# The second MLP in three 768-token tiles, both of its products by block sums

## Chip, cores and metric

One core of one Trainium2 chip runs the kernel. The time is device microseconds of the whole kernel, from one launch, and its median over the runs; less is better. TensorE multiplies, VectorE, ScalarE and GpSimd work on elements, SyncE issues the DMAs.

## What is computed

Windowed attention over 4 sequences of 576 positions and 8 heads, then two MLPs of width 512 and inner width 2048 over all 2304 tokens:

```python
x = attention(q, k, v).transpose(0, 2, 1, 3).reshape(2304, 512)
h = x @ w_in;  r = max(h, 0);  x = (r * r) @ w_out            # first MLP
h = x @ w2_in; g = h * (1 / (1 + exp(-h))); out = g @ w2_out  # second MLP
```

All of it has to hold to nearly 32-bit precision. The weights arrive as 64-bit floating point, and the kernel itself turns them into 32-bit.

## The kernel before

**Precision.** TensorE multiplies in a rounded 32-bit type. Each operand is therefore split into a rounded part (hi, a cast) and the remainder (lo, a subtraction), and a product is three matmuls: hi x hi, hi x lo, lo x hi.

**Block sums.** In the first product of an MLP, `mlp2` (line 971) takes 512 tokens and two 128-row blocks of the inner width (a pair f, eight pairs in all) as a 2 x 2 by 2 x 2 block product and forms it from seven products of block sums instead of eight products of blocks. The blocks and sums of the weights are called a11, a12, a22 and s1 to s4, those of the tokens b11, b21, b22 and t1 to t4. Each of the seven is 2 x 3 matmuls of 256 columns (line 999). The seven lie in four banks of PSUM, and VectorE and ScalarE add them up into a tile `h` (lines 1013 and 1015). A 256-token tile takes eight plain products instead.

**Second product.** After a pair's sums come the nonlinearity (lines 1035 to 1041), the split of `g` (lines 371 and 378) and, one pair later, the plain second product: per block c 12 matmuls of the tile's whole width (lines 1053 to 1055), which accumulate over all sixteen blocks in four banks y0 to y3.

**Tiles and stages.** The first MLP has three tiles of 256 tokens (beside attention) and three of 512, the second four of 512 and one of 256. `weights` (line 381) converts one block of weights: load, six or so element operations (lines 405 to 441), split. `sums` (line 466) forms s1 to s4. Blocks and sums of the first product go to DRAM and are streamed back for every tile by `stream` (line 512); the second product's weights stay in sixteen resident buffers `w1`. `load_x` (line 919) loads and splits a tile's tokens and forms t1 to t4 (line 966).

**Order.** A planner (`Planner.order`) simulates five engines with fixed costs and gives every operation its engine and its place in that engine's queue, by a key (a due time in units of one block for 256 tokens). All DMAs go through SyncE's queue in the planned order; a DMA that waits for a buffer holds up those behind it. SBUF is handed out in pages: 28 of 4 KB per partition (`u4`), 8 and 2 of 2 KB, beside the sixteen `w1` and two `blk`.

Of the kernel before, what the change touches and what calls it, by code (L numbers as in the profile page):

```python
# [27 lines left out]
P = 128  # L28
# [12 lines left out]
HOLDS = {"w0": "u4", "wa": "u4", "ws": "u4", "wb": "u4", "wc": "u2", "h": "u4", "xr": "u4", "xo": "u2", "cw": "u2", "raw": "u4", "ap": "u4", "x": "u4", "x2": "u4", "xn": "u2", "g4": "u4", "st": "u4",  # L41
         "g2": "u2", "cv": "u2", "r": "u3", "yo": "u2", "stg": "u2"}
# [40 lines left out]

class Buf:


    def __init__(self, tags, make, psum):
        self.tags, self.make, self.psum = tags, make, psum
        self.alloc_op = self.tile = self.pages = None
        self.last = {}  # L90
# [13 lines left out]
class Op:  # L104
    def __init__(self, engines, fn, deps, key, allocs, uses):
# [6 lines left out]
        self.pace, self.full, self.lock, self.kind = False, True, False, 0  # L112
# [4 lines left out]
class Planner:  # L117
# [7 lines left out]
    def __init__(self):  # L125
        self.ops, self.slots = [], {}

    def buf(self, tags, make, psum=False):

        for g, n in tags.items():  # L130
            self.slots.setdefault(g, [Page() for _ in range(n)])
        return Buf(list(tags), make, psum)
# [10 lines left out]
    def order(self):  # L143
        after, left, users = {}, {}, {}
        pace = sorted((o for o in self.ops if o.pace), key=lambda o: o.key)
        for o in self.ops:
# [3 lines left out]
            need = set(o.deps)  # L150
# [6 lines left out]
        slots = self.slots  # L157
# [10 lines left out]
        def at(o, e, t):  # L168
            for g, k in o.wants:
                x = [p.free.get(e, 0.0) for p in slots[g] if not p.held]  # L170
                if len(x) < k:
                    return None
                t = max(t, min(x) if k == 1 else sorted(x)[k - 1])
# [12 lines left out]
        def take(b, e):  # L186
            b.pages = [min((p for p in slots[g] if not p.held), key=lambda p: p.free.get(e, 0.0)) for g in b.tags]
            for p in b.pages:
                p.held = True

        def drop(b):
            f = {e: max(t + self.SYNC[x, e] for x, t in b.last.items()) for e in free}
            for p in b.pages:
                p.held, p.free = False, f

# [17 lines left out]
        def fill(until):  # L213

            while free["PE"] + 0.25 < until:
# [10 lines left out]
                take(b, "PE")  # L226
# [11 lines left out]
        while left_n:  # L238
# [32 lines left out]
            for b in o.allocs:  # L271
                take(b, e)
# [48 lines left out]
class Kern:  # L321
    def __init__(self, ctx, tc, qkv, w1, w2, out):
# [3 lines left out]
        self.sb = pool("sb")  # L326
        self.ps = pool("ps", space=bass.MemoryType.PSUM)
        self.dr = pool("dr", space=bass.MemoryType.DRAM)
        self.pl = Planner()
# [8 lines left out]

    def buf(self, tag, bufs, cols, dt=F32, rows=P):
        return self.pl.buf({tag: bufs}, lambda: self.sb.tile([rows, cols], dt, tag=tag, name=tag, bufs=bufs))  # L340

    def spot(self, use, cols, dt=F32):

        pool, most = HOLDS[use], MOST[use]
        bufs, words = POOLS[pool]
        words //= 2 if dt == I64 else 1
        return self.pl.buf({use: most, pool: bufs}, lambda: self.sb.tile(
            [P, words], dt, tag=pool, name=use, bufs=bufs)[:, :cols])
# [32 lines left out]
    def weights(self, m, c, key, dkey, js=(0, 1)):  # L381
# [3 lines left out]
        for j in js:  # L385
            raw = self.spot("raw", n, I64)
            cv = self.spot("cv", n)
# [939 lines left out]
```

## Time and profile before

| | |
|---|---|
| median of 3 runs | 891.92 us (890.57 to 892.31) |
| span of the profiled execution | 894.6 us |
| TensorE busy, share of the span | 875.7 us, 98% |
| VectorE | 647.2 us, 72% |
| ScalarE | 425.0 us, 48% |
| GpSimd | 107.9 us, 12% |
| moved by DMA | 217.33 MB, 243 GB/s |

The span is that of the execution that was profiled, from its first to its last instruction; that execution's own time outside the profiler is not given, and the median is that of other runs. The second MLP begins at about 502 us. A matmul's row is longer than the distance to the next one, since matmuls overlap; the pace is read from the distance between starts.

### The profile page before, as it was taken

The page shows a single profiled execution, that of the slowest core. Times are in us where ns is not written, and L with a number is a line of the kernel's source. Part 1 is how long each engine was busy: PE and PEld are TensorE (multiplying, and loading weights), DVE is VectorE, ACT ScalarE, POOL GpSimd, SP SyncE. Part 2 cuts the span into 40 slices and gives each one's busy share as a digit, 9 for nine tenths or more (in the row PEclk, how much of TensorE's full clock was granted, in tenths as well). Part 3 has the DMA queues.
Part 4 walks back from the last instruction along what each step waited for, and adds up shares of the span by engine and source line. Part 5 has one row for each costly group of instructions (what it writes and reads, how often), then busy time and mean ns, then how long its engine had stood idle before and what let it go on. Part 6 is the DMA issues. An engine that isn't in the chain of part 4 may idle for free.

```text
span 894.6 us, 17795 instructions
## 1 busy us (share of the span) xinstructions
PE 875.7 (98%) x6511; PEld 798.8 (89%) x6511; DVE 647.2 (72%) x1652; ACT 425.0 (48%) x1113; POOL 107.9 (12%) x125
## 2 busy tenths in 40 slices
PE   8999999999989999999999999999999999999998
PEld 6889899999877888989999988999999999999998
DVE  7999999788786997776788999684557445545322
ACT  5978888777455365432333364342233222323222
POOL 2242233111311010010110012000002000000000
PEclk9999999999999999999999999999999999999999
DMA  6887685579898988966787897956575556634050
GB/s 259 279 268 270 212 308 200 193 273 323 287 301 310 340 322 299 346 213 238 235 282 260 329 329 268 325 196 236 165 240 206 172 188 219 260 141 164 25 212 25
DMA packets 75735, 217.33 MB, mean 243 GB/s; under 512 B 8576, under 2 KB 20096, under 8 KB 75648
## 3 DMA queue, kind: packets, MB, share of 16 engines
q1 hardware_dynamic: 75648, 216.20, 69.2%
q8 instruction: 51, 0.84, 0.4%
q14 instruction: 36, 0.29, 0.1%
HBM read 170.03 MB, written 46.14 MB: 242 GB/s over the span
## 4 chain that ended last, share of the span: by engine, by line
PE 68%; DVE 16%; DMA 7%; issue 4%; ACT 3%; POOL 1%; SPq 0%; DVEq 0%; POOLq 0%; ACTq 0%
PE s L999 28%; PE y L1053 10%; PE y L1054 10%; PE y L1055 10%; DMA raw<-w 4%; DVE ap L625 2%; DMA x<-xo 1%; DVE cv L441 1%; DVE g L378 1%; PE s L851 1%; DVE cv L437 1%; DVE h L1015 1%; PE s L853 1%; PE s L852 1%; DVE w L378 1%
## 5 line engine op out<-in xcount | busy, mean ns | idle before, releaser
L1015 DVE TENSOR_TENSOR h<-s,h 128x512 f32<-128x512 f32 x224 | 139.4, 622 | 127.5 <-PE s L999 117.1
L1053 PE MATMUL y<-g,w 128*128 128x512 f32 (+1 forms) x512 | 194.7, 380 | 1.1 <-ACT yo L371 1.0
L1054 PE MATMUL y<-g,w 128*128 128x512 f32 (+1 forms) x512 | 192.8, 377 | 1.0 <-DVE g L378 1.0
L1055 PE MATMUL y<-g,w 128*128 128x512 f32 (+1 forms) x512 | 192.7, 376 | 0.0
L999 PE MATMUL s<-x,ws 128*128 128x256 f32 x1344 | 171.9, 283 | 0.1
L999 PEld LDWEIGHTS s<-x,ws 128*128 128x128 f32 x1344 | 165.8, 192 | 0.7 <-DVE h L1015 0.3
L371 ACT CAST g<-r 128x512 fp32r<-128x512 f32 (+1 forms) x175 | 94.1, 542 | 72.4 <-DVE r L1035 41.9
L378 DVE TENSOR_TENSOR g<-r,g 128x512 fp32r<-128x512 f32 (+1 forms) x172 | 102.8, 613 | 21.8 <-ACT g L371 18.3
L1055 PEld LDWEIGHTS y<-g,w 128*128 128x128 f32 x512 | 96.2, 188 | 18.3
L1053 PEld LDWEIGHTS y<-g,w 128*128 128x128 f32 x512 | 96.2, 188 | 17.4 <-ACT yo L371 1.6
L1054 PEld LDWEIGHTS y<-g,w 128*128 128x128 f32 x512 | 96.3, 188 | 16.4 <-DVE g L378 1.3
L999 PEld LDWEIGHTS s<-x,wa 128*128 128x128 f32 x768 | 99.8, 191 | 5.8 <-ACT xo L371 1.1
L999 PE MATMUL s<-x,wa 128*128 128x256 f32 x768 | 103.8, 284 | 1.0 <-ACT xo L371 0.9
L1039 ACT ACTIVATE r<-h 128x512 f32<-128x512 f32 x64 | 37.1, 624 | 121.5 <-DVE h L1015 121.4
L633 ACT ACTIVATE ap<-ap,ast 96x128 f32<-96x128 f32 (+3 forms) x168 | 61.8, 370 | 19.0 <-DVE ast L625 18.9
L427 POOL TENSOR_SCALAR raw<-raw 128x512 f32<-128x512 f32 x40 | 39.2, 982 | 179.1 <-ACT cv L405 88.7
L1013 ACT COPY h<-s 128x256 f32<-128x256 f32 x56 | 20.8, 371 | 80.8 <-PE s L999 79.0
L851 PE MATMUL s<-x,w 128*128 128x256 f32 x192 | 57.1, 297 | 0.2 <-DVE ast L625 0.2
L1041 DVE TENSOR_TENSOR r<-h,r 128x512 f32<-128x512 f32 x64 | 41.7, 687 | 20.2 <-ACT r L1039 20.2
L852 PE MATMUL s<-x,w 128*128 128x256 f32 x192 | 54.7, 285 | 0.2 <-DVE x L378 0.2
L853 PE MATMUL s<-x,w 128*128 128x256 f32 x192 | 54.5, 284 | 0.0
L413 ACT ACTIVATE raw<-raw 128x512 int32<-128x512 uint32 x59 | 40.2, 681 | 25.2 <-DMA raw<-w 25.1
(144 smaller groups left out, 1442.5 us busy)
## 6 DMA issues: line engine op xcount, KB each, us to landing
raw<-w SPq DMA_DIRECT2D x64, 512.0 KB, 6.1
ws<-w2x SPq DMA_DIRECT2D x64, 512.0 KB, 5.3
ws<-w1x SPq DMA_DIRECT2D x48, 512.0 KB, 6.0
wa<-w2s SPq DMA_DIRECT2D x40, 512.0 KB, 4.5
wa<-w1s SPq DMA_DIRECT2D x24, 512.0 KB, 5.9
w1s<-w SPq DMA_DIRECT2D x16, 512.0 KB, 4.1
w1x<-st SPq DMA_DIRECT2D x16, 512.0 KB, 3.4
w2s<-st SPq DMA_DIRECT2D x16, 512.0 KB, 4.8
```

Of the source, the lines that this page charges most:

```text
L371: self.nc.scalar.copy(out=out, in_=in_)
L378: self.eng[eng].tensor_tensor(out=out, in0=a, in1=b, op=ALU.subtract)
L633: es.append(self.op({"ACT": c_act(nk) + 0.185}, lambda e, i=i, n=n, c=c, p=p, st=st: nc.scalar.activation(out=p.tile[:n, c], in_=p.tile[:n ...
L851: nc.tensor.matmul(o, wh.tile[:, s], xh, start=(kk == 0), stop=False)
L852: nc.tensor.matmul(o, wh.tile[:, s], xl, start=False, stop=False)
L853: nc.tensor.matmul(o, wl.tile[:, s], xh, start=False, stop=(kk == KC - 1))
L999: nc.tensor.matmul(bank.tile[:, o:o + 256], wp, xp, start=i == 0, stop=last, skip_group_check=True)
L1015: add = lambda o, a, b: nc.vector.tensor_tensor(out=o, in0=a, in1=b, op=ALU.add)
L1041: b = self.op({"DVE": c_dve(n)}, lambda e, r=r, src=src: nc.vector.tensor_tensor(out=r.tile, in0=src(), in1=r.tile, op=ALU.mult), [a], k, ...
L1053: nc.tensor.matmul(o, wh.tile[:, s], gh.tile, start=c == 0, stop=False)
L1054: nc.tensor.matmul(o, wh.tile[:, s], gl.tile, start=False, stop=False)
L1055: nc.tensor.matmul(o, wl.tile[:, s], gh.tile, start=False, stop=(c == NF - 1))
```

## The change

The second MLP runs in three tiles of 768 tokens, in blocks of 384. Its second product is formed from seven products too. A tile is two phases (`strassen`, new): first the first product of all eight pairs, each with its nonlinearity, into sixteen buffers `gq`; then the second product, one of the seven products after the other, each over all eight pairs. The seven no longer lie apart and are added up outside: products chain in their bank. A2 goes on in A1's bank after A1's result has been copied out, A3 and A4 after that, B2 in B1's; what has to be added from another bank is added on the way out. The block sums of `g` are formed in place in the second phase, and each is split just ahead of its product into one of ten buffers `hl`.

The second product's weights are converted with a narrower first block, over about twice the stretch; their sums s1 to s4 are formed (`sums2`, new), stored to DRAM and streamed back in every tile (`stream2`, new); a11, a12 and a22 stay resident (`wp`). `load_xs` (new) loads and splits the tokens of a 768-token tile and forms the differences in place. SBUF is one area in pieces of 256 words (`Area`, `put`), where the new buffers get any free place, from its low or its high end. The keys of the second MLP's weight conversions are set anew.

```diff
-TILES = ([(0, 256), (256, 256), (512, 256), (768, 512), (1280, 512), (1792, 512)], [(0, 512), (512, 512), (1024, 512), (1536, 512), (2048, 256)])
-
-POOLS = {"u4": (28, 1024), "u2": (8, 512), "u3": (2, 512)}
+TILES = ([(0, 256), (256, 256), (512, 256), (768, 512), (1280, 512), (1792, 512)], [(0, 768), (768, 768), (1536, 768)])
+POOLS = {"u2": (8, 512), "u3": (2, 512), "u4": (28, 1024), "w1": (16, 1024), "blk": (BLK_BUFS, 1280)}
...
+    def put(self, place, dt, name):
+
...
+        if at > self.ring_at:
+            self.ring.tile([P, at - self.ring_at], F32, name="gap")
+        self.ring_at = at + words
+        return self.ring.tile([P, words // (2 if dt == I64 else 1)], dt, name=name)
...
+            late = m and j
+            wide = n if not late or c % 2 else n // 2
             both = (self.spot("st", 2 * n, F32R) if m and not j else self.spot("w0", 2 * n, F32R) if j == 0 else
-                    self.buf("w1", NF, 2 * n, F32R))
+                    self.spot("wp" if c < 2 * KEPT else "sq", 2 * wide, F32R) if late else self.buf("w1", NF, 2 * n, F32R))
...
+            if late:
+                f = c // 2
+                names = ("a12", "a22") if c % 2 else ("a11",)
+                if f < KEPT:
+                    for i, name in enumerate(names):
+                        self.wp[name, f] = (Part(both, 512 * i, 256), Part(both, 512 * i + 256, 256), [h, r])
...
+                self.cv[c] = (cv, w)
+                if c % 2:
+                    self.sums2(f, k)
+                continue
...
+    def sums2(self, f, key):
+
...
+        a = lambda i, j: Part((ca, cb)[j], 256 * i, 256)
+        s = [self.spot("st", 2 * PIECE, F32R) for _ in range(2)]
+        part = [Part(s[i // 2], 512 * (i % 2) + 256, 256) for i in range(4)]
+        what = [(a(1, 0), a(1, 1), ALU.add), (part[0], a(0, 0), ALU.subtract),
...
+            o = self.op({"DMA": c_dma(P * PIECE * 8)}, lambda e, q=q: nc.sync.dma_start(
+                out=self.w2y[2 * q:2 * q + 2, f].rearrange("i p n -> p i n"),
...
+            for i in range(2):
+                self.kept[f"s{2 * q + i + 1}", f] = o
+
...
+    def stream2(self, name, f, key):
+
+        b = self.spot("sw", 1024, F32R)
+        i = (PLAIN).index(name)
+        o = self.op({"DMA": c_get(P * 4096)}, lambda e: self.nc.sync.dma_start(
+            out=b.tile.bitcast(F32).rearrange("p (f n) -> p f n", f=2),
+            in_=self.w2y[i, f:f + 2].rearrange("f p n -> p f n")), [self.kept[name, f], self.kept[name, f + 1]], key, [b])
+        o.gate, o.behind, self.last_sw = key, self.last_sw, o
...
+    def load_xs(self, m, t, key):
...
+        def less(i, a, b, deps, key):
+            return self.op({"Pool": c_pool2(n), "DVE": c_dve(n)}, lambda e: self.sub(e, v(i), v(a), v(b)), deps, key, [], raw, None, True)
+
+        k = key + 4
+        b11 = keep("b11", 0, got[:2], k)
+        t1 = less(0, 1, 0, b11, k + 1)
+        d1 = keep("t1", 0, [t1], k + 2)
+        b21 = keep("b21", 2, got[2:], k + 3)
+        t2 = less(0, 3, 0, d1 + got[2:], k + 4)
+        d2 = keep("t2", 0, [t2], k + 5)
+        keep("b22", 3, got[2:], k + 6)
+        t3 = less(1, 3, 1, [t1] + got[2:], k + 7)
+        keep("t3", 1, [t3], k + 8)
+        t4 = less(2, 2, 0, b21 + d2, k + 9)
+        keep("t4", 2, [t4], k + 10)
...
+    def strassen(self, m, t, k0, fetched):
...
+        lists = {"A1": ("a11", "b11"), "B1": ("s1", "t1"), "C1": ("a12", "b21"), "A2": ("s2", "t2"),
+                 "B2": ("s4", "b22"), "A3": ("s3", "t3"), "A4": ("a22", "t4")}
...
+        def move(out, bank, deps, key, allocs, uses):
+            return self.op({"ACT": c_actp(half)}, lambda e: nc.scalar.copy(out=out(), in_=bank.tile[:, :half]),
+                           deps, key, allocs, uses + [bank])
+
+        def plus(out, bank, deps, key, uses):
+            return self.op({"DVE": c_dve(half)}, lambda e: add(out(), bank.tile[:, :half], out()), deps, key, [], uses + [bank])
+
+        for f in range(nf + 1):
+            for at, (name, late) in enumerate((("A1", 0), ("B1", 0), ("A3", 1), ("C1", 0), ("A2", 0), ("A4", 1), ("B2", 0))):
+                q = f - late
+                if not 0 <= q < nf:
+                    continue
+                key = k0 + unit * f + 0.4 * at
+                a, b = lists[name]
+                new = name[1] == "1"
+                if new:
+                    y = ("sa", "sa") if not t and not q else (f"y{q % 2 * 2}", f"y{q % 2 * 2 + 1}")
+                    banks[name[0], q] = self.bank({"A": y[0], "B": y[1], "C": "sa"}[name[0]])
+                bank = banks[name[0], q]
+                w = fetched[q][a]
+
+                def s1(e, bank=bank, w=w, b=b, new=new):
+                    o = bank.tile[:, :half]
+                    for kk in range(2):
+                        for part in range(3):
+                            nc.tensor.matmul(o, w[part == 2].tile[:, kk * P:kk * P + P], x[b][part == 1].tile[:, kk * half:kk * half + half],
+                                             start=new and not kk and not part, stop=kk == 1 and part == 2, skip_group_check=True)
+
+                before = {"A2": ["c1"], "A3": ["c2"], "A4": ["c22"], "B2": ["c5"]}.get(name, [])
+                chain = self.op({"PE": 6 * c_mm(half)}, s1, [chain, w[2]] + x[b][2] + [done[i, q] for i in before], key,
+                                [bank] if new else [], [w[0].whole, x[b][0].whole] + ([] if new else [bank]))
+                chain.tagname = f"S1.{m}.{t}.{q}.{name}"
...
+                if name == "A1":
+                    g[q] = [self.spot("gq", n) for _ in range(2)]
...
+                lo, hi = g[q]
+                if name == "A1":
+                    done["c1", q] = move(p(0), bank, [chain], k, [lo], [])
+                elif name == "B1":
+                    done["c5", q] = move(p(3), bank, [chain], k, [hi], [])
+                elif name == "C1":
+                    done["c11", q] = plus(p(0), bank, [chain, done["c1", q]], k, [lo])
+                elif name == "A2":
+                    done["c2", q] = move(p(1), bank, [chain], k, [], [hi])
+                elif name == "B2":
+                    done["c12", q] = plus(p(1), bank, [chain, done["c2", q]], k, [hi])
+                elif name == "A3":
+                    done["c22", q] = plus(p(3), bank, [chain, done["c5", q]], k, [hi])
+                else:
+                    done["c21", q] = move(p(2), bank, [chain], k, [], [lo])
+                for i, (what, of) in enumerate((("A4", ("c11", "c21")), ("A3", ("c12", "c22")))):
+                    if name != what:
+                        continue
+                    b = g[q][i]
+                    deps = [done[o, q] for o in of]
...
+                    r = self.spot("sg", n)
+                    d = self.op({"ACT": c_act(n)}, lambda e, r=r, b=b: nc.scalar.activation(
+                        out=r.tile, in_=b.tile, func=AF.Sigmoid), deps, k + 0.2, [r], [b])
+                    done["g", i, q] = self.op({"DVE": c_dve(n)}, lambda e, r=r, b=b: nc.vector.tensor_tensor(
+                        out=b.tile, in0=b.tile, in1=r.tile, op=ALU.mult), [d], k + 0.3, [], [r, b], None, True)
...
+        k0 += unit * nf
...
+        order = [("A1", 0), ("B1", 0), ("A2", 0), ("B2", 3), ("A3", 1), ("C1", 2), ("A4", 2)]
+        steps = []
+        for at, (name, i) in enumerate(order):
+            if ends and name == "A4":
...
+                steps += [(at + q / nf, name, i, (0, 1), q) for q in range(nf)]
+        steps.insert(nf + 1, steps.pop(nf - 1))
...
+            if (name, q) not in halves:
+                lim = key - HL_LEAD
+                p = lambda i, q=q: g[q][i % 2].tile[:, i // 2 * half:i // 2 * half + half]
+                of = {"B1": (0, 1, 0), "A2": (0, 3, 0), "A3": (1, 3, 1), "A4": (2, 2, 0)}.get(name)
+                if of:
+                    o, u, v = of
+                    d = self.op({"DVE": c_dve(half), "Pool": c_pool2(half)}, lambda e, p=p, o=o, u=u, v=v: self.sub(e, p(o), p(u), p(v)),
+                                ready[o, q] + ready[u, q] + ready[v, q], lim, [], g[q], None, True)
...
+                hl = self.spot("hl", n, F32R)
...
+                behind = h
+                h = self.op({"ACT": c_act(half)}, lambda e, p=p, i=i, hi=hi: self.copy(e, hi.tile, p(i)), ready[i, q], lim, [hl], [g[q][i % 2]])
+                h.behind = behind
+                l = self.op({"DVE": c_dve(half), "Pool": c_pool2(half)}, lambda e, p=p, i=i, hi=hi, lo=lo: self.sub(
+                    e, lo.tile, p(i), hi.tile.bitcast(F32)), [h], lim, [], [g[q][i % 2], hl], None, True)
...
+            def s2(e, ch=ch, q=q, hi=hi, lo=lo, wh=wh, wl=wl, bank=bank, new=new):
+                for c in ch:
+                    o = bank[c].tile[:, :half]
+                    for part, (u, v) in enumerate(((wh, hi), (wh, lo), (wl, hi))):
+                        nc.tensor.matmul(o, u.tile[:, c * P:c * P + P], v.tile, start=new and not q and not part,
+                                         stop=q == nf - 1 and part == 2, skip_group_check=True)
+
+            own = new and first
+            prev = self.op({"PE": 3 * len(ch) * c_mm(half)}, s2,
+                           [prev, hd, ld] + wd + ([done[u, c] for u in before for c in range(2)] if first else []), key,
+                           bank if own else [], [wh.whole, hl] + ([] if own else bank))
...
+            if name == "C1":
+                self.s1_last = prev
...
+                if name in ("C1", "A3", "B2", "A4"):
+                    e0, a0 = blk // 2 * 2 + c, t0 + blk % 2 * half
+                    self.ydone[m, t, e0, blk % 2] = self.op({"DMA": c_dma(P * half * 4)}, lambda e, o=o, e0=e0, a0=a0: nc.sync.dma_start(
+                        out=(self.y1, self.out)[m][e0][:, a0:a0 + half], in_=o()), [d], k + 0.1, [], [y[blk]])
...
+        for c in range(NF):
+            k = end + W2B_FROM + W2B_STEP * c
+            self.weights(1, c, k, k - 4, (1,))
...
-                for c in range(NF):
-                    self.weights(1, c, k + 2 * c + W2_BACK, k + 2 * c + W2_BACK - 4, (1,))
-                self.load_x(1, 0, end - X_LEAD)
...
+                self.load_xs(1, 0, end - X_LEAD)
             self.mlp2(0, t, k, ahead(0, t))
+        self.shared = False
         for t in range(len(TILES[1])):
-            k = start(1, t)
+            k, u = start(1, t), unit[1][t]
             if t + 1 < len(TILES[1]):
-                self.load_x(1, t + 1, k + 4)
-            self.mlp2(1, t, k, ahead(1, t))
+                self.load_xs(1, t + 1, k + u * NF - X2_LEAD)
+            got = [self.stream(1, f, k + u * f - S_AHEAD, True) for f in range(NF // 2)]
+            for at, name in enumerate(("a11", "s1", "s2", "s4", "s3", "a12", "a22")):
+                for f in range(0, NF // 2, 2):
+                    if name in SUMS or f >= KEPT:
+                        self.stream2(name, f, k + u * NF / 2 + u * (NF / 2) / 7 * (at + f / 8) - S2_AHEAD)
+            self.strassen(1, t, k, got)
...
+KEPT = 8
+SUMS = ("s1", "s2", "s3", "s4")
+PLAIN = SUMS + ("a11", "a12", "a22")
+W2B_FROM = -36.97
+W2B_STEP = 3.69
+X2_LEAD = 12.31
+S_AHEAD = 9.18
+S2_AHEAD = 11.24
+HL_LEAD = 4.48
...
-X_LEAD = 25.91
+X_LEAD = 24.75
...
-W2_BACK = 10.73
...
-W2_FROM = 50.0
-W2_STEP = 5.76
-W2_SPLIT = 12
-W2_LATE = 6.0
-W2_LSTEP = 3.76
+W2_FROM = 48.22
+W2_STEP = 6.77
+W2_SPLIT = 14
+W2_LATE = 3.74
+W2_LSTEP = 4.34
```

## Rows read from the trace of the kernel before

**Rows 1.** The page: busy time, and the chain that ended last by engine and line
```profile
PE 875.7 (98%) x6511; PEld 798.8 (89%) x6511; DVE 647.2 (72%) x1652; ACT 425.0 (48%) x1113; POOL 107.9 (12%) x125
...
PE s L999 28%; PE y L1053 10%; PE y L1054 10%; PE y L1055 10%; DMA raw<-w 4%; DVE ap L625 2%; DMA x<-xo 1%; DVE cv L441 1%; DVE g L378 1%; PE s L851 1%; DVE cv L437 1%; DVE h L1015 1%; PE s L853 1%; PE s L852 1%; DVE w L378 1%
```

**Rows 2.** Busy time by stage: stretch, length, engines, granted clock, DMA share, GB/s
```profile
600.00:840.00 240.00, 240.00 (x1509) 218.00 (x1508) 124.84 (x196) 70.12 (x128) 6.35 (x7) 1.00 0.55 191
```

**Rows 3.** Chain that ended last, two periods of a 512-token tile: start, us, what
```profile
609.11 5.03 PE s L999 x42
...
630.10 5.03 PE s L999 x42
```

**Rows 4.** The same chain, the last 256-token tile
```profile
865.50 2.87 PE s L999 x24
...
882.68 2.87 PE s L999 x24
```

**Rows 5.** Timeline of TensorE: the second MLP's first and the kernel's last matmul
```profile
501.71 1.60 PE L999 MATMUL s<-x,wa 128*128 128x256 f32 x12
...
890.97 0.28 PE L1055 MATMUL y<-g,w 128*128 128x256 f32 x1
```

**Rows 6.** What TensorE waited for, 500 to 895 us: total, times, longest
```profile
PE y L1054 <- DVE g L378: 1.0, 1, 1.0
PE y L1053 <- ACT yo L371: 0.3, 1, 0.3
```

**Rows 7.** Groups of matmuls by form, 600 to 890 us: busy us, mean ns
```profile
L1053 PE MATMUL y<-g,w 128*128 128x512 f32 x192 | 75.0, 390 | 0.0
...
L999 PE MATMUL s<-x,ws 128*128 128x256 f32 x552 | 70.0, 283 | 0.0
```

**Rows 8.** Timeline of VectorE, back to back: start, us, operation
```profile
530.07 0.68 DVE L378 TENSOR_TENSOR w<-cv,w 128x512 fp32r<-128x512 f32 x1
530.67 0.42 DVE L1015 TENSOR_TENSOR h<-s,h 128x256 f32<-128x256 f32 x1
531.00 0.68 DVE L378 TENSOR_TENSOR x<-blk,x 128x512 fp32r<-128x512 f32 x1
```

**Rows 9.** Timeline of ScalarE, back to back
```profile
515.98 0.63 ACT L371 CAST w<-cv 128x512 fp32r<-128x512 f32 x1
516.50 0.39 ACT L1013 COPY h<-s 128x256 f32<-128x256 f32 x1
516.76 0.70 ACT L413 ACTIVATE raw<-raw 128x512 int32<-128x512 uint32 x1
```

**Rows 10.** Timeline of GpSimd, two two-input operations
```profile
542.56 0.75 POOL L493 TENSOR_TENSOR st<-cv 128x256 f32<-128x256 f32 x1
543.25 0.75 POOL L493 TENSOR_TENSOR st<-cv,st 128x256 f32<-128x256 f32 x1
```

**Rows 11.** Busy time by stretch, columns as in rows 2
```profile
300.00:500.00 200.00, 199.36 (x1333) 179.10 (x1332) 161.91 (x334) 77.93 (x182) 18.20 (x27) 1.00 0.80 276
500.00:510.00 10.00, 10.00 (x66) 9.12 (x65) 9.83 (x18) 3.40 (x6) 1.42 (x3) 1.00 1.01 393
510.00:540.00 30.00, 29.17 (x186) 25.96 (x184) 27.98 (x49) 19.57 (x35) 5.95 (x5) 1.00 0.87 322
540.00:590.00 50.00, 49.36 (x305) 44.61 (x306) 38.50 (x65) 19.68 (x37) 4.41 (x6) 1.00 0.88 310
```

**Rows 12.** DMA issues, 500 to 895 us: KB each, median us to landing
```profile
ws<-w2x SPq DMA_DIRECT2D x58, 512.0 KB, 5.1
wa<-w2s SPq DMA_DIRECT2D x37, 512.0 KB, 4.2
wc<-w2s SPq DMA_DIRECT2D x29, 256.0 KB, 4.4
out<-yo SPq DMA_DIRECT2D x16, 256.0 KB, 2.3
...
out<-yo SPq DMA_DIRECT2D x4, 128.0 KB, 1.7
```

More of the change, by code (lines that the diff above doesn't have):

```diff
@@ L81, in __init__, with times, take, drop @@
         self.held, self.free = False, {}
+class Area:
+    def __init__(self):
+        self.at, n = {}, 0
+        for g, (bufs, words) in POOLS.items():
+            self.at[g] = (n, bufs, words // GRAIN)
+            n += bufs * words // GRAIN
+        self.size, self.stamp, self.known = n, 0, {}
+        self.free = {e: np.zeros(n) for e in ("PE", "ACT", "DVE", "Pool", "DMA")}
+    def times(self, tag, e):
+        key = (tag, e)
+        if self.known.get(key, (-1,))[0] != self.stamp:
+            f = self.free[e]
+            if tag in self.at:
+                o, n, k = self.at[tag]
+                t = f[o:o + n * k].reshape(n, k).max(1)
+            else:
+                t = np.lib.stride_tricks.sliding_window_view(f[tag[3]:tag[4]], tag[1]).max(1)
+            self.known[key] = (self.stamp, t, np.sort(t[t < 1.0e8]).tolist())
+        return self.known[key]
+    def take(self, tag, e, t):
+        x = self.times(tag, e)[1]
+        if tag in self.at:
+            o, n, k = self.at[tag]
+            at = o + k * int(x.argmin())
+        else:
+            fit = np.flatnonzero(x <= max(t, x.min()) + 1.0e-9)
+            k, at = tag[1], tag[3] + int(fit[0] if tag[2] == "lo" else fit[-1])
+        for f in self.free.values():
+            f[at:at + k] = 1.0e9
+        self.stamp += 1
+        return at, k
+    def drop(self, place, free):
+        at, k = place
+        for e, f in self.free.items():
+            f[at:at + k] = free.get(e, 0.0)
+        self.stamp += 1
 class Buf:
@@ L88, in __init__ @@
         self.tags, self.make, self.psum = tags, make, psum
[L89 removed]
+        self.alloc_op = self.tile = self.pages = self.places = None
         self.last = {}
@@ L111, in __init__ @@
         self.start = self.end = self.eng = self.gate = None
-        self.pace, self.full, self.lock, self.kind = False, True, False, 0
+        self.pace, self.full, self.lock, self.kind, self.behind = False, True, False, 0, None
         for b in allocs:
@@ L184, in vacant, with take @@
             return min([p.free.get(e, 0.0) for p in slots[g] if not p.held], default=1.0e9)
-        def take(b, e):
-            b.pages = [min((p for p in slots[g] if not p.held), key=lambda p: p.free.get(e, 0.0)) for g in b.tags]
+        def take(b, e, t):
+            b.pages = [min((p for p in slots[g] if not p.held), key=lambda p: p.free.get(e, 0.0)) for g in b.tags if g in slots]
             for p in b.pages:
                 p.held = True
+            b.places = [area.take(g, e, t) for g in b.tags if g not in slots]
         def drop(b):
@@ L194, in drop @@
                 p.held, p.free = False, f
+            for p in b.places:
+                area.drop(p, f)
         cover, state = {}, [False]
@@ L344, in spot @@
         pool, most = HOLDS[use], MOST[use]
[L345 to L348, printed above, removed]
+        if pool in POOLS:
+            tags = {use: most, pool: POOLS[pool][0]}
+        else:
+            lo, hi = (SHARED_LO, SHARED_HI) if self.shared else (0, self.pl.area.size - 1)
+            tags = {use: most, ("free", -(-cols // GRAIN), pool, lo, hi): 1}
+        b = self.pl.buf(tags, lambda: self.put(b.places[0], dt, use)[:, :cols])
+        return b
     def bank(self, use):
```

167 lines of the change are left out of this document (147 added, 20 removed).

## Prediction

> **What bounds the kernel now.** I read the page first: TensorE is busy 98% of the span, and of the chain that ended last 28% lie on the block products (line 999) and 10% on each of the three lines of the second products [rows 1]. Then the busy time by stage: in the second MLP's steady part TensorE is busy 240.00 of 240 us while VectorE does 124.84 and the DMA engines stand at 0.55 [rows 2]. There every matmul that goes is time gone. The granted clock is 1.00, that is 2.4 GHz.
>
> Next the pace. In the chain a 512-token tile repeats every (630.10 - 609.11) / 2 = 10.495 us (two periods), of which 5.03 us are the 42 block matmuls of 256 columns and 5.465 us the 24 of 512 columns [rows 3]. That is 0.1198 and 0.2277 us for one. The 256-token tile repeats every (882.68 - 865.50) / 3 = 5.727 us (three periods) [rows 4]. The second MLP is 4 tiles x 8 x 10.495 = 335.8 us and 8 x 5.727 = 45.8 us, together 381.6 us of matmul pace. Its first matmul starts at 501.71 and its last at 890.97 [rows 5]; 389.4 us lie between, 5.5 of them belong to the first MLP's last 24 matmuls, so 2.2 us are waits. The waits that the profile names are 1.3 us [rows 6]. After the last matmul 3.5 us remain to the span's end at 894.6.
>
> **Matmuls removed and added.** Before: 4 x (336 of 256 columns + 192 of 512) + 384 of 256 = 1728 of 256 and 768 of 512, 835,584 columns. After: three tiles of 768, blocks of 384 columns; the first product has 8 x 7 x 6 = 336 matmuls, the second 7 products x 8 row pairs x 2 output blocks x 3 = 336. In all 2016 of 384 columns, 774,144 columns. No 384-column matmul is in the trace. Its neighbours are 0.1198 and 0.2277, and their rows are 283 and 390 ns long, 107 ns apart for 256 columns [rows 7]: a fixed part plus a part per column. So I take the middle, 0.1737 us, and 2016 x 0.1737 = 350.3 us: **31.3 us less**. Bounds: priced per column like the 512 one (0.2277 x 0.75 = 0.1708) 344.3 us, 37.3 less; like the 256 one (0.1198 x 1.5 = 0.1797) 362.3 us, 19.3 less.
>
> The fixed part is 2 x 0.1198 - 0.2277 = 0.0119 us by these rows. The Trainium skill, "TensorE: Matmul & The Clock Gate", section "Back-to-back issue gap", puts the warm gap at N / 2.4 + 2.5 ns. An estimate by it is 354.4 us before and 327.6 after, 26.8 less; the trace disagrees, since it shows 381.6 us for the first of the two.
>
> **Work of the other engines in a new tile.** A tile is now two phases of 336 x 0.1737 = 58.4 us; a product of six matmuls is 1.04 us. VectorE starts run 0.60 us apart at 512 columns and 0.33 at 256 [rows 8], so I take 0.47 for 384 and 0.86 for 768. ScalarE: 0.52 and 0.26 [rows 9], so 0.40 and 0.79.
> First phase, per pair of weight blocks: three additions of 384 and two products of 768 on VectorE (3.1 us), four copies and two sigmoids on ScalarE (3.2 us), within 7.3 us: 43%. Second phase: 56 remainders and 32 differences of 384, six sums into the output, and the next tile's four differences and seven remainders of 768: 94 x 0.47 + 11 x 0.86 = 53.6 us of 58.4 if GpSimd takes none of them. That is 92%; ScalarE has 56 casts and 8 copies of 0.40 and seven casts of 0.79, 31.1 us, and is hidden beside it. GpSimd does a two-input operation of 256 in 0.69 us [rows 10], so it can take some. Cover: up to ten buffers of prepared halves. The nearest row for so full a VectorE is 510 to 540 us: 27.98 of 30 us busy, TensorE 29.17 [rows 11]. That prices it at 0 to 0.8 us per 30 us.
>
> **Where the wait moves.** Chaining means that a product goes on into the bank of an earlier one, so TensorE waits until a copy or an addition has read that bank. What is queued behind is all of TensorE. In the first phase A2 has three products between (3.1 us) and a copy of 0.40 to wait for; the tightest is A4 behind the addition that follows A3, with two products between (2.1 us) against 0.47 us plus what VectorE has ahead (a 768 product is 0.86). Hidden while VectorE is less than about 1.3 us late; the row on the nearest wait, TensorE on a VectorE remainder, is one of 1.0 us [rows 6]. In the second phase eight row pairs (8.3 us) lie between. The seam between the phases: the last pair needs a copy, a sigmoid, a product, a cast and a remainder, 0.40 + 0.79 + 0.86 + 0.40 + 0.47 = 2.9 us and four hand-overs; the A1 product's last pair is put behind two pairs of B1, so nine pairs, 9.4 us, cover it.
>
> **Second weights.** Removed: the conversion into resident 512-column pairs and its place beside the last first-MLP tile. Added per weight pair: four sums of 256 and two remainders of 512 on VectorE or GpSimd (4 x 0.34 + 2 x 0.60 = 2.6 us), two casts of 512 on ScalarE, two stores of 512 KB; 16 stores in all, on SP's queue like every load, so a load issued later stands behind them. The even blocks get 256 instead of 512 columns of cast and remainder (8 x 0.26 us less). The key of each conversion spreads the sixteen over twice the time, the last six into the first phase of the first new tile. There VectorE has 25 us of its own and about eight conversions (four operations of 0.60, 2.4 us) plus four times 2.6 us of sums, 54 of 58 us: 93%, as in 510 to 540 us. For the stretch I keep the old 2.2 us of waits; none to 8 us are the ends. In the first MLP itself TensorE is busy 199.36 of 200 us from 300 to 500 [rows 11], so the spread can give back 0.6 us at most and, with VectorE at 161.91 of 200, should cost nothing: 0, ends -0.6 and +2.
>
> **Loads.** A pair of first-product weights is 512 + 256 + 2 x 512 KB [rows 12] = 1.835 MB; a tile needs 14.7 MB in 58.4 us = 251 GB/s, and the sums of the second product another 8.4 MB per tile, mostly in the second phase. Before, the steady tiles drew 191 GB/s [rows 2], which is what it asked for and no ceiling. In the first new tile's first phase: 9.2 MB of stream (three pairs are ahead), 4.2 of raw weights, 3.1 of stores of sums, 2.1 of late first weights, 3.7 of sums ahead = 22.3 MB, 382 GB/s. The rows show 393 GB/s for 10 us, 322 for 30 and 310 for 50 [rows 11]. At 322 it is 69 us, 11 late; without the sums ahead, which that phase doesn't use, 18.6 MB and 58 us, not late. I take not late.
> The Trainium skill, "DMA: Bandwidth & Descriptors", section "Where 436 GB/s comes from", has about 358 GB/s for loads from HBM on one core; an estimate by it is 62 us, 4 late. The 10 us at 393 GB/s stand above it.
>
> **Smaller edits.** The tail: the last output transfers are 192 KB, between 128 KB (1.7 us) and 256 KB (2.3 us) [rows 12], and the copy is 384 instead of 256 columns: +0.4 us, ends 0 and +1. The warm-up matmul keeps 256 columns and the planner's places are decided ahead of the run: 0. Buffers now lie wherever room is; by the limits of the code gates, inputs, kept weights and stream fill 186 of 206 pieces of 256 words late in a first phase, so loads may start later. This costs nothing while three pairs stay ahead; its price is among the rivals.
>
> **Sum.** -31.3; waits from 2.2 to 6.0 (2.2 for the first phase of the first tile, 0.8 for each second phase, 0.35 for each of four other seams), +3.8; tail +0.4. That is -27.1. The profiled span goes from 894.6 to 867.5; the median of the runs shown is 2.7 us below that span, and 891.9 - 27.1 = **864.8 us**.
>
> **Rivals.** *Transfers late in the first new tile:* 4 to 11 us, so 869 to 876; for it the 382 GB/s, against it that sums can wait. 0.15. *VectorE answers late*, in A4's wait and in the differences of B1 and A2, which follow each other (0.94 us of VectorE per 1.04 us): 1 to 4 us per tile, 866 to 876; for it the 92%, against it GpSimd and the lead. 0.14. *The fixed part does not shrink with the number of matmuls*, so only 61,440 columns go, at (0.2277 - 0.1198) / 256 = 0.42 ns, 25.9 us: 870. 0.03. (By the gap of the Trainium skill named above it would be 869, an estimate.) *A 384-column matmul costs per column* as the shorter one does: 877. 0.04. *No added wait at all*: 859 to 861; 0.10. *Slower than before*: full memory keeps the stream from running ahead, and each first phase is bound by transfers. It loses the whole gain when three phases grow by 27.1 us, 9.0 each: 14.7 MB in 67.4 us, below 218 GB/s. Rows of 310 and 322 GB/s with TensorE losing 1.5 of 80 us speak against; for it, 251 GB/s is asked for with less room than now. At 191 GB/s: 76.9 us a phase, 55 us more, 920. 0.05, of which 0.01 near no change. The forecast itself, 861 to 868: 0.49.
>
> **Range and chances.** 857 takes in the low price of the matmul with the waits (891.9 - 37.3 + 4.2 = 858.8); 876 the late transfers and VectorE. Outside are the stream-bound case, the high price and a little of each late case, some 0.13. A difference under 0.2% (1.8 us) cannot be told from no change here. Faster 0.95, same 0.01, slower 0.04.
>
> **What would show it.** Matmul rows of 384 columns, 2016 of them, about 337 ns long, starts 0.174 us apart, a product every 1.04 us, a first-phase pair every 7.3 us, a tile every 117 us. TensorE's waits in the second MLP about 6 us. If transfers are late, TensorE waits for a weight tile right after the first MLP; if VectorE is, TensorE waits on it with VectorE above 95% in second phases. The prediction is wrong if 384 columns take other than 0.171 to 0.180 us, or if waits exceed 17 us.

## The result, and the profile after

The changed kernel takes 863.83 us in the median of 4 runs (863.07 to 865.18), the kernel before 892.07 (890.57 to 892.31). The ratio is 0.968, with a 95% interval of 0.964 to 0.971: 28.2 us less. On a second chip it was 865.02 against 893.20, again 28.2 us less. Forecast were 27.1 us less and 864.8 us.

| | before | after |
|---|---|---|
| span of the profiled execution | 894.6 us | 861.5 us |
| TensorE busy | 875.7 us, 98% | 844.0 us, 98% |
| VectorE | 647.2 us, 72% | 713.7 us, 83% |
| ScalarE | 425.0 us, 48% | 504.7 us, 59% |
| GpSimd | 107.9 us, 12% | 102.8 us, 12% |
| moved by DMA | 217.33 MB | 227.77 MB |

Less work on TensorE, more on every other engine but GpSimd: that is the trade. The page of the changed kernel, busy time and two of the costliest groups (line, engine, operation, count, busy us, mean ns), answers [rows 1, 7]:

```profile
PE 844.0 (98%) x6031; PEld 797.7 (93%) x6031; DVE 713.7 (83%) x1808; ACT 504.7 (59%) x1255; POOL 102.8 (12%) x108
...
L1292 PE MATMUL y<-xs,ws 128*128 128x384 f32 x552 | 106.9, 334 | 0.0
L1380 PE MATMUL sa<-hl,wp 128*128 128x384 f32 x432 | 77.5, 335 | 1.1 <-ACT hl L446 0.9
```

Line 1292 is the first product, line 1380 the second. A 384-column matmul's row is 334 to 335 ns long, close to midway between 283 and 390. The pace answers [rows 3]; the chain in the second tile, start, us, what:

```profile
641.34 6.24 PE y L1292 x36
647.58 1.04 PE sa L1292 x6
648.62 6.24 PE y L1292 x36
654.86 1.04 PE sa L1292 x6
```

A pair takes 654.86 - 647.58 = 7.28 us for 42 matmuls, 0.1733 us for one, with nothing between. Busy time by half tile, in the order first and second phase of each tile, the last with the kernel's end (stretch, length, TensorE, weight loads, VectorE, ScalarE, GpSimd, granted clock, DMA share, GB/s), answers [rows 2, 11]:

```profile
512.00:570.30 58.30, 58.30 (x338) 58.16 (x337) 51.33 (x95) 38.10 (x68) 1.57 (x2) 1.00 0.82 297
570.30:628.60 58.30, 57.25 (x329) 56.67 (x328) 50.43 (x92) 33.35 (x66) 4.32 (x3) 1.00 0.83 286
628.60:686.90 58.30, 58.30 (x338) 58.30 (x337) 34.45 (x56) 31.12 (x53) 0.00 (x0) 1.00 0.63 224
686.90:745.10 58.20, 58.20 (x338) 58.20 (x337) 49.01 (x89) 31.19 (x63) 4.88 (x4) 1.00 0.68 230
745.10:803.00 57.90, 57.90 (x336) 57.90 (x335) 34.05 (x56) 31.13 (x53) 0.00 (x0) 1.00 0.64 217
803.00:861.50 58.50, 54.67 (x316) 54.35 (x314) 38.47 (x77) 26.94 (x57) 1.01 (x1) 1.00 0.31 108
```

TensorE is full in four of the first five and misses 1.05 us in the other. The only wait of 0.1 us or more that the profile names for it from 490 us on, answers [rows 6]:

```profile
PE sa L1380 <- ACT hl L446: 0.9, 1, 0.9
```

In TensorE's timeline the second MLP's first matmul starts at 500.49 and the kernel's last at 856.29 + 6 x 0.1733 = 857.33 (the last row holds seven). With the last matmul's own 0.17 these are 357.0 us. 5.5 of them belong to the first MLP's last 24 matmuls, 349.4 are 2016 x 0.1733, and about 2.2 are waits, as many as before.

```profile
500.49 1.23 PE L1292 MATMUL sa<-xs,wa 128*128 128x384 f32 x6
...
856.29 1.38 PE L1380 MATMUL sa<-hl,wp 128*128 128x384 f32 x7
```

**Two spans, one caution.** The spans differ by 33.1 us and the medians by 28.2. Every run's time on record lies about 1.8 us above its span, so the execution of before that was profiled took some 896.4 us, more than any other of that kernel on record (890.2 to 896.15). A further execution of the same first MLP (the kernel of the first experiment below) starts its second MLP at 497.81 us and not at 501.71 [rows 5]. So against that row the changed kernel's first MLP ends 2.7 us later (500.49; a second execution of the changed kernel has 501.35), and not 1.2 us earlier. With 2.7 the account is: first MLP +2.7, matmuls 381.6 - 349.4 = -32.2, waits 2.2 as before, the end (after the last matmul) 3.5 to 4.0 = +0.5: -29.0 us, against 28.2 measured. The 2.7 rests on one execution of the old first MLP. A second way to it: from the second MLP's start to the span's end the two profiles have 392.9 and 361.0 us, 31.9 less, so the 28.2 of the medians leave 3.7 for what stands before.

### The profile page after: what moved, and what is told of

Same layout as the page of the kernel before. It is cut to its first block, busy times and chain, and to the rows that moved or that the text cites. A ratio compares the mean times of both kernels' runs of the same rounds, so it can differ in the third digit from the quotient of the medians.

```text
span 861.5 us, 17138 instructions
## 1 busy us (share of the span) xinstructions
PE 844.0 (98%) x6031; PEld 797.7 (93%) x6031; DVE 713.7 (83%) x1808; ACT 504.7 (59%) x1255; POOL 102.8 (12%) x108
## 2 busy tenths in 40 slices
DMA packets 85653, 227.77 MB, mean 264 GB/s; under 512 B 8768, under 2 KB 22336, under 8 KB 85568
## 4 chain that ended last, share of the span: by engine, by line
PE 80%; DMA 3%; DVE 3%; ACT 1%; issue 1%; POOL 0%; SPq 0%; DVEq 0%; POOLq 0%; ACTq 0%
PE y L1292 17%; PE sa L1380 14%; PE s L1134 13%; PE y L1380 6%; PE y L1188 5%; PE y L1189 5%; PE y L1190 5%; PE sa L1292 4%; DMA blk<-qkv 2%; PE s L986 1%; PE ax L826 1%; PE ax L736 1%; PE s L988 1%; PE s L987 1%; PE ax L804 1%; PE y L1034 1%
## 5 line engine op out<-in xcount | busy, mean ns | idle before, releaser
L446 ACT CAST hl<-gq 128x384 fp32r<-128x384 f32 x168 | 80.6, 514 | 53.1 <-PE sa L1380 21.7
L453 DVE TENSOR_TENSOR hl<-gq,hl 128x384 fp32r<-128x384 f32 x168 | 91.9, 580 | 18.7 <-ACT hl L446 18.4
L1292 PE MATMUL y<-xs,ws 128*128 128x384 f32 x552 | 106.9, 334 | 0.0
L1292 PEld LDWEIGHTS y<-xs,ws 128*128 128x128 f32 x552 | 96.7, 188 | 0.0
L1380 PE MATMUL sa<-hl,wp 128*128 128x384 f32 x432 | 77.5, 335 | 1.1 <-ACT hl L446 0.9
L1380 PEld LDWEIGHTS sa<-hl,wp 128*128 128x128 f32 x432 | 75.0, 188 | 1.6 <-ACT hl L446 1.2
L1188 PE MATMUL y<-g,w 128*128 128x512 f32 x192 | 76.4, 398 | 0.0
L1134 PE MATMUL s<-x,ws 128*128 128x256 f32 x576 | 75.1, 284 | 0.0
L1189 PE MATMUL y<-g,w 128*128 128x512 f32 x192 | 75.1, 391 | 0.0
L1190 PE MATMUL y<-g,w 128*128 128x512 f32 x192 | 74.8, 390 | 0.0
L1134 PEld LDWEIGHTS s<-x,ws 128*128 128x128 f32 x576 | 71.4, 192 | 0.2
L1150 DVE TENSOR_TENSOR h<-s,h 128x512 f32<-128x512 f32 x96 | 59.5, 620 | 13.9 <-PE s L1134 8.2
## 6 DMA issues: line engine op xcount, KB each, us to landing
raw<-w SPq DMA_DIRECT2D x64, 512.0 KB, 6.0
ws<-w1x SPq DMA_DIRECT2D x48, 512.0 KB, 6.5
ws<-w2x SPq DMA_DIRECT2D x48, 512.0 KB, 5.4
sw<-w2y SPq DMA_DIRECT2D x48, 512.0 KB, 5.2
wa<-w1s SPq DMA_DIRECT2D x24, 512.0 KB, 5.9
wa<-w2s SPq DMA_DIRECT2D x24, 512.0 KB, 5.3
w1s<-w SPq DMA_DIRECT2D x16, 512.0 KB, 4.4
w1x<-st SPq DMA_DIRECT2D x16, 512.0 KB, 3.5
```

Of the source, the lines that this page charges most:

```text
L446: self.nc.scalar.copy(out=out, in_=in_)
L453: self.eng[eng].tensor_tensor(out=out, in0=a, in1=b, op=ALU.subtract)
L1134: nc.tensor.matmul(bank.tile[:, o:o + 256], wp, xp, start=i == 0, stop=last, skip_group_check=True)
L1188: nc.tensor.matmul(o, wh.tile[:, s], gh.tile, start=c == 0, stop=False)
L1189: nc.tensor.matmul(o, wh.tile[:, s], gl.tile, start=False, stop=False)
L1190: nc.tensor.matmul(o, wl.tile[:, s], gh.tile, start=False, stop=(c == NF - 1))
```

## Experiments

Differences are to the kernel before on the same chip. The changed kernel is 28.2 us below it on two chips; "against the change" means against that.

**Is there a fixed part per matmul?** In the kernel before, the second MLP's plain second product in halves:

```diff
-nc.tensor.matmul(o, wh.tile[:, s], gh.tile, start=c == 0, stop=False)
...
+parts = [slice(0, 256), slice(256, 512)] if m and n == 512 else [slice(0, n)]
...
+    for h in parts:
+        nc.tensor.matmul(o[:, h], u.tile[:, s], v.tile[:, h], ...
```

> The kernel before, with each 512-column matmul of the second MLP's plain second product cut into two of 256: the same columns, 768 matmuls more. Theory (a matmul costs a fixed 0.0119 us beside its columns, from the two paces of before): 768 x 0.0119 = 9.1 us more, about 901. Rival (the fixed part is some 2.5 ns): 1.9 us more, about 894. Rival (cost goes by columns alone): no change.

Measured 901.85 against 893.41 us, ratio 1.010 (1.007 to 1.013): 8.4 us more for 768 matmuls and not one column more. The chain shows the period directly; the last line, from TensorE's timeline, is the second MLP's first matmul in this kernel:

```profile
617.22 5.04 PE s L999 x42
628.01 5.04 PE s L999 x42
...
497.81 1.60 PE L999 MATMUL s<-x,wa 128*128 128x256 f32 x12
```

10.79 instead of 10.495 us [rows 3], 0.295 for 24 more matmuls, 0.0123 each. The fixed part of 0.0119 us holds. The Trainium skill ("TensorE: Matmul & The Clock Gate", "Back-to-back issue gap") gives 2.5 ns beside the columns for an isolated matmul's gap; an estimate by it is 1.9 us. This run, a stream of matmuls with a weight load each, disagrees.

**Is TensorE the bound in the second phases?** Eight products instead of seven there:

```diff
+if new and v8:   # v8: name == "A1"
+    for u, v in ((wh, hi), (wh, lo), (wl, hi)):
+        nc.tensor.matmul(o, u.tile[:, c * P:c * P + P], v.tile, ...)
```

> The changed kernel with the A1 product of every second phase done twice, so that it has eight products instead of seven as a plain block product would (the output is then not the reference's); 144 matmuls of 384 columns more. Theory (TensorE is the bound in the second phases): 144 x 0.1733 = 25.0 us more, about 889. Rival (VectorE or the transfers set the second phases' pace): clearly less, 0 to 15 us more.

Measured 891.44 us, ratio 0.998 (0.996 to 1.000): 26.2 us more against the change, where 25.0 are the matmuls. In the profiled execution the second MLP is 25.2 us longer, and the rest lies before it. This one product out of eight is nearly the whole gain: with eight products in its second phase the new tiling would be within 2 us of the kernel before.

**Where is the next bound?** The third matmul of each product left out in the second phases:

```diff
-for part, (u, v) in enumerate(((wh, hi), (wh, lo), (wl, hi))):
+for part, (u, v) in enumerate(((wh, hi), (wh, lo))):
```

> The changed kernel without the third matmul of each product (remainder of the weights by rounded values) in the second phases, 336 of 1008 matmuls fewer there (the output is less exact). It shows the next bound. Theory (VectorE needs 47 to 54 us of the 58.4 of a second phase): the phase shrinks to that and not to TensorE's 38.9, so 13 to 34 us less, about 840. Rival (TensorE alone is the bound and VectorE far from it): 3 x 19.4 = 58 us less, about 806.

Measured 833.08 us, ratio 0.934 (0.930 to 0.938): 32.1 us less against the change, 10.7 per second phase, and not 19.4. A stretch of which the last 30 us lie in the first tile's second phase, columns as above:

```profile
560.00:600.00 40.00, 36.69 (x197) 35.21 (x197) 38.16 (x78) 26.70 (x56) 0.62 (x1) 0.96 0.79 279
```

VectorE is at 95%, ScalarE at 67%, and TensorE waits on the casts and remainders (8.4 and 6.7 us in all). A second phase can shrink from 58.3 to about 48 us before VectorE takes over.

**How much more can VectorE take?** In A1, B2 and C1 the remainder is computed twice:

```diff
+if name in ("A1", "B2", "C1"):
+    l = self.op({"DVE": ..., "Pool": ...}, ...)   # the remainder again
```

> The changed kernel with the remainder of three of the seven products of a second phase (A1, B2, C1) computed twice: 24 x 0.47 = 11.3 us more for VectorE in each second phase, where it is busy 50.4, 49.0 and (of 54) 38.5 us of 58.3. Theory (VectorE has 8 to 9 us of room there, so it becomes the bound in the first two tiles only, by 2 to 4 us each): 3 to 8 us more, about 870. Rival (VectorE already sets the pace): the whole 34 us more, 898. Rival (room is ample, through GpSimd and buffers): no change.

Measured 869.25 us against 865.02 of the changed kernel beside it, ratios 0.973 (0.970 to 0.976) and 0.970 (0.965 to 0.974): 4.2 us more, though the two intervals overlap. The three second phases:

```profile
570.30:628.60 58.30, 55.27 (x309) 54.69 (x308) 54.01 (x109) 30.10 (x62) 18.26 (x3) 0.97 0.79 271
...
686.90:745.10 58.20, 57.96 (x334) 57.64 (x333) 55.06 (x109) 31.14 (x63) 18.39 (x3) 1.00 0.65 220
...
803.00:860.00 57.00, 56.77 (x327) 56.45 (x327) 50.21 (x104) 28.48 (x60) 6.35 (x1) 1.00 0.31 105
```

The loss is in the first tile alone: TensorE misses 3.0 us at a granted clock of 0.97, where it missed 1.05. In the second tile VectorE stands at 95% and TensorE misses 0.24 us. GpSimd's row goes to 18 us, but not because it did more: it has three operations, as before or one fewer, and a two-input one now takes 6.4 to 9.6 us beside the fuller VectorE, where it took 1.0 to 2.1. Part of the next tile's preparation moved on into the first phases of the second and third tile, where VectorE is busy 38.7 and 37.8 us instead of 34.5 and 34.1.

**What is the chain's wait worth?** A4 right behind A3, so that no product of the first phase covers the addition between them:

```diff
-(("A1", 0), ("B1", 0), ("A3", 1), ("C1", 0), ("A2", 0), ("A4", 1), ("B2", 0))
+(("A1", 0), ("B1", 0), ("A3", 1), ("A4", 1), ("C1", 0), ("A2", 0), ("B2", 0))
```

> The changed kernel with A4 put right behind A3 in the first phase, so that no product covers the addition that has to read the bank between them. Theory (the chain's wait is real and was covered by two products): per pair the end of the matmul, the addition of 0.47 and two hand-overs, about 0.9 us, 24 pairs, 20 us more, about 884. Rival (the wait never mattered, the cover is worth nothing): no change, 864. If it costs much more, VectorE is often behind when A3 ends.

Measured 879.30 us, ratio 0.984 (0.981 to 0.987): 14.1 us more against the change. That is about two thirds of the forecast, and the account behind it falls. What TensorE waited for, and its timeline at the second tile's seam:

```profile
PE sa L1380 <- ACT hl L446: 6.0, 3, 2.0
PE y L1292 <- DVE gq L1263: 2.8, 4, 0.9
PE sa L1292 <- DVE gq L1263: 0.7, 1, 0.7
...
698.20 1.21 PE L1380 MATMUL y<-hl,sw 128*128 128x384 f32 x6
701.45 2.31 PE L1380 MATMUL sa<-hl,wp 128*128 128x384 f32 x6 [2.04 <-ACT hl L446]
703.55 7.46 PE L1380 MATMUL y<-hl,sw 128*128 128x384 f32 x36
```

The uncovered wait is 0.9 us at most, as estimated, but it occurs five times and not 24. In most pairs the planner had put a product of the second phase (A1, of a pair that was ready) between A3 and A4. Those products are then missing where the phases meet, and there TensorE waits 2 us per tile for the last pair's cast. The clock adds to it: after the wait six matmuls take 2.10 us, 0.35 each, and the stretch from 700 to 710 us has a granted clock of 0.83. So the chain's cover is needed, and moving it uncovers the seam.

**Are the transfers near their edge?** Copies of 512 KB from DRAM to DRAM beside each pair's loads in the first phases, one per pair, three per pair, one in the later tiles only, one in the first tile only:

```diff
+scr = self.dr.tile([P, 2 * PIECE], F32, name=f"scr{t}_{f}_{i}")
+o = self.op({"DMA": c_dma(P * 4096)}, lambda e, ...: self.nc.sync.dma_start(
+    out=scr, in_=self.w2s[2 * f + i % 2]), ..., k + u * f - S_AHEAD + 0.5)
```

> The changed kernel with one more transfer per weight pair in every first phase, a DRAM to DRAM copy of 512 KB: 4.2 MB read and written more per phase of 58.3 us, where 297, 224 and 217 GB/s are moved now. Theory (transfers are covered with room): within 2 us of the changed kernel. Rival (the stream is at its edge, above all in the first tile): 4 to 11 us more.

> As before with three such copies per pair: 12.6 MB more per first phase, 29.9 MB in the first tile and some 25.6 in the others. Theory (a ceiling between 322 and 393 GB/s as in the rows of before): the phases become bound by transfers, 18 to 35 us late in the first tile and 7 to 21 in each other, 30 to 75 us more. Rival (the ceiling is higher, or copies cost less than loads): under 10 us more.

> The changed kernel with one extra 512 KB copy per pair in the first phases of the second and third tile only. There 224 and 217 GB/s become about 290 to 314. Theory (only the first tile's transfers are at their edge): no change, within 2 us of 864. Rival (each first phase is near its edge): 3 to 6 us more.

> The changed kernel with the same copies in the first tile's first phase only, 4.2 MB on top of 17.3 MB. Theory (all that the copies in all three tiles cost, 8.9 us, arises here): 8 to 10 us more, about 873. Rival (the copies cost a third in each tile): 3 us more.

| copies | us | ratio to before (95%) | against the change |
|---|---|---|---|
| one per pair, all tiles | 873.96 | 0.980 (0.977 to 0.984) | +9.0 |
| three per pair, all tiles | 923.68 | 1.033 (1.030 to 1.037) | +58.7 |
| one per pair, later tiles | 864.45 | 0.969 (0.967 to 0.971) | -0.2 |
| one per pair, first tile | 874.44 | 0.979 (0.976 to 0.982) | +9.8 |

So the expectation of no cost was wrong for the first tile and right for the others, whose first phases move 287 and 283 GB/s with one copy per pair and lose nothing. With three copies TensorE waits for the seam after the first MLP (15.0 us), for ScalarE's casts in the second phases (12.5 us) and for `ws` and `wa` tiles (5.6 and 3.8 us), and the kernel is slower than the one before. Of the waits for tiles 5.0 us lie in the second and third tile, so the transfers bind there too, but most of the loss is in the first. That is the slow rival's outcome, reached with 12.6 MB more per first phase.

**Is it the bytes in the first tile?** The same copies at 256 KB, and at 512 KB with the loads of the second product's sums due later in that tile:

```diff
-... * (at + f / 8) - S2_AHEAD)
+... * (at + f / 8) - (S2_AHEAD if t else 3.0))
```

> As before with copies of 256 KB, 2.1 MB in all in the first tile's first phase. Theory (that phase moves 297 GB/s and saturates at about 313, so it has 0.9 MB of room): 1.2 MB too many, 3 to 5 us more. Rival (there is no room at all, cost in proportion): 4.5 us; with more room than thought: under 1 us.

> The 512 KB copies in the first tile's first phase, and the loads of the second product's sums in that tile due 3 instead of 11.24 key units ahead, so that up to 3.7 MB of them leave the first phase. Theory (the rate of all transfers is what binds, and these loads can wait): most of the 9 us comes back, 864 to 867. Rival (the late part is the order of SyncE's queue or the conversions' own chain, not the sum of bytes): 871 to 875.

Measured 874.47 us, ratio 0.979 (0.976 to 0.982), and 874.98, ratio 0.981 (0.978 to 0.984). Half the bytes cost as much as all, 9.9 us against the change where 3 to 5 were expected. The second edit eased nothing, because there was nothing to ease: three loads of those sums, and not 3.7 MB, fall into the first tile's first phase without it, and three still do. DMA issues from 512.0 to 570.3 us, the changed kernel, then the run with the loads due later:

```profile
sw<-w2y SPq DMA_DIRECT2D x3, 512.0 KB, 4.9
...
sw<-w2y SPq DMA_DIRECT2D x3, 512.0 KB, 3.8
```

So the reading that the sum of bytes is not the cause rests on the 256 KB run alone, which moves 17.58 MB in that stretch where the changed kernel moves 17.31. The timeline at the seam from the first MLP to the second, with the 256 KB copies, shows where it is lost; ScalarE, then TensorE:

```profile
511.05 0.62 ACT L446 CAST st<-st 128x512 fp32r<-128x512 f32 x1 [1.20 <-DVE st L615]
512.68 1.07 ACT L446 COPY yo<-y 128x512 f32<-128x512 f32 x2 [1.01 <-DVE st L615]
515.38 1.26 ACT L446 COPY yo<-y 128x512 f32<-128x512 f32 x2 [1.63 <-DMA y<-yo]
...
516.02 2.29 PE L1292 MATMUL y<-xs,wa 128*128 128x384 f32 x6 [4.45 <-ACT yo L446]
518.11 2.12 PE L1292 MATMUL y<-xs,ws 128*128 128x384 f32 x6
520.03 2.09 PE L1292 MATMUL sa<-xs,ws 128*128 128x384 f32 x6
521.95 1.22 PE L1292 MATMUL sa<-xs,wa 128*128 128x384 f32 x6
```

Each engine works in its planned order. VectorE sat 1.8 us until a raw weight load landed (2.4 us with the 512 KB copies in the first tile). Behind that conversion come the weight sums `st`. ScalarE stands at their cast, and behind the cast are the copies that empty the first MLP's output banks. Between these copies ScalarE waits another 1.63 us for the store of a first copy to land. TensorE waits for those banks. In the changed kernel the same copies run at 509.39 and 510.83 us and TensorE goes on at 511.48.

Which load came late can be read from SyncE's queue, the changed kernel, then the one with the 256 KB copies:

```profile
487.61 1.51 SPq L475 DMA_DIRECT2D raw<-w  x2
...
496.65 1.31 SPq L625 DMA_DIRECT2D w2y<-st  x2
...
499.14 0.41 SPq L475 DMA_DIRECT2D raw<-w  x1
...
488.36 0.33 SPq L475 DMA_DIRECT2D raw<-w  x1
...
496.81 0.94 SPq L625 DMA_DIRECT2D w2y<-st  x2
...
500.67 0.86 SPq L475 DMA_DIRECT2D raw<-w  x2
```

In the changed kernel two raw loads stand ahead of the two stores of weight sums, which are issued at 496.65 us. With the copies one of the two stands behind them and is issued some 11 us later. It is so in all four kernels with one copy per pair in the first tile, at 512 KB as at 256, and in none of the seven profiled executions of kernels with the change and no copies there. The planner also gives VectorE the operation that waits for a raw load here (line 485), where the changed kernel has ScalarE wait for one (line 483):

```profile
504.48 0.68 ACT L483 ACTIVATE cv<-raw 128x512 f32<-128x512 f32 x1 [0.77 <-DMA raw<-w]
...
506.64 0.43 DVE L485 TENSOR_SCALAR cv<-raw 128x512 f32<-128x512 f32 x1 [1.77 <-DMA raw<-w]
```

So the copies changed the order in which the planner places loads and operations, and the loss at the seam can be followed back to that order. That a want of room for bytes has no part in it is argued from the 256 KB run and not shown, and that this one load's place alone makes the loss was not tried. The seam is not all of it: with the 512 KB copies in the first tile TensorE waits 3.1 us there, and about as much goes in the first tile's second phase, where VectorE is fuller (columns as above; the changed kernel, then that run):

```profile
570.00:628.00 58.00, 56.95 (x327) 56.37 (x326) 50.24 (x93) 33.35 (x66) 4.32 (x3) 1.00 0.83 286
...
570.00:628.00 58.00, 53.72 (x297) 52.52 (x296) 54.77 (x104) 32.73 (x66) 5.76 (x4) 0.97 0.75 266
```

## Why the prediction was right

**The price of a matmul** carried it: 0.1737 us forecast, 0.1733 measured; 31.3 us forecast, 32.2 measured. Reading two widths as a fixed part plus a part per column was the decisive step, and the first experiment confirms the fixed part by itself. The price per column (19.3 or 37.3 us) is excluded, and so is the rival that the fixed part doesn't shrink with the count (25.9).

**TensorE as the bound** held on both sides: 25.0 us of matmuls more cost 26.2, and 58 fewer gave 32, where VectorE took over.

**VectorE in the second phases**: 53.6 us forecast if GpSimd takes nothing; 50.4 and 49.0 were busy, with 4.3 and 4.9 on GpSimd. In the first tile's first phase 54 forecast, 51.3 measured. The rival "VectorE answers late" did not happen: at 84 to 87% busy no wait of TensorE on VectorE of 0.1 us or more is named; by the shortened product the room is some 10 us a phase.

**Waits** were over-sized: 6.0 forecast, about 2.2 measured. The allowance of 0.8 for each second phase was taken from a stretch where VectorE was at 93%, the 0.35 for each seam has no row behind it, and nearly none of either came.

**Transfers in the first tile**: not late, as taken, but by wrong steps. 382 GB/s were said to be asked for if all went ahead; 297 were moved, 17.3 MB and not 22.3. Of the sums ahead, taken as 3.7 MB, three loads of 512 KB fell into that phase, and the rest of the difference lay outside it too. The rival's size (4 to 11 us) comes with copies of 2.1 MB in all just as with 4.2, with a changed order of the loads, and by these runs not through the rate.

**The first MLP** was taken as untouched, 0 with ends of -0.6 and +2. Against the further execution of the old one it is about 2.7 us longer, 3.7 by the medians, outside those ends. The rows show where: from 200 to 250 us TensorE is busy 45.48 us in the changed kernel and 49.31 with the old first MLP, and waits on attention's loads and small operations (4.4 us of named waits against 0.6). In the next 50 us it makes up 1.0 of it.

```profile
200.00:250.00 50.00, 45.48 (x439) 41.93 (x438) 40.85 (x149) 32.42 (x120) 2.95 (x3) 1.00 0.85 289
...
200.00:250.00 50.00, 49.31 (x433) 45.51 (x432) 42.85 (x130) 29.56 (x96) 11.24 (x11) 1.00 0.91 314
```

The first row is the changed kernel's, the second that of the first experiment. The step that failed is pricing the re-keyed conversions from the full stretch 300 to 500 us alone; they start before it, beside attention. That it is the conversions and not the new places in SBUF was not tried. **The tail** was +0.5, forecast +0.4. The errors (waits -3.8, first MLP +2.7, price -0.9) partly cancel, so the total is closer than its terms, and that part is luck.

## What to carry to other kernels

Where one engine is full, price a change by that engine's instructions at the pace between starts, split into a fixed part and a part per column from two widths; fewer, wider instructions count beside fewer columns. Chaining results in a bank cost nothing here while two other products lay between, but cover is a stock: used in one place, it is missing at the seam. And a stage that shows no wait can still stand at an edge: what sits in an ordered queue in front of the copies that free the banks decides it, and the average rate doesn't show it. When an experiment adds work to a planned kernel, read first whether the plan stayed the same.

## What the runs showed of the hardware

After a wait TensorE can go on at the lower of its two clock levels for a while. After 4.45 us of waiting, three products ran at 0.320 to 0.348 us per matmul at a granted clock of 0.50, which is 384 columns at 1.2 GHz, before the pace was 0.173 again; the wait of 4.45 us cost some 3 more. After a wait of 2.04 us six matmuls took 0.35 each. The length of the wait alone does not settle it: after 3.06 us at the seam with the 512 KB copies in the first tile the granted clock stayed at 1.00, as it did after the one wait of 0.9 us in the changed kernel. With three copies per pair, the long waits at the seam show a granted clock of 0.73 and then 0.50 (busy time by stretch, columns as before):

```profile
512.00:524.00 12.00, 1.31 (x6) 0.75 (x4) 0.86 (x2) 0.59 (x1) 0.00 (x0) 0.73 1.01 388
524.00:530.00 6.00, 1.73 (x5) 1.73 (x6) 2.88 (x6) 0.59 (x1) 0.00 (x0) 0.50 0.47 178
```
